# Nine pairs of row tiles multiplied by one level of Strassen, in a newly searched order

## The chip, the cores and the metric

The kernel runs on one core of one Trainium2 chip. The metric is device time in microseconds: the median of the runs of one kernel. The core has five engines that run their own instruction streams and wait for one another by semaphores: TensorE (PE, matmuls, with the weight load shown apart as PEld), VectorE (DVE), ScalarE (ACT), GpSimd (POOL) and SyncE (SP), whose queue issues the DMAs.

## The reference

Linear attention over 8 batches, 8 heads, 576 rows and 64 columns a head, followed by a feed-forward layer on the 4608 rows of 512 columns.

```python
q_s = exp(q - max(q, -1)); q_s = q_s / (sum(q_s, -1) + 1e-09)
k_s = exp(k - max(k, 2));  k_s = k_s / (sum(k_s, 2) + 1e-09)
kv  = einsum('bhsd,bhse->bhde', k_s, v)
x   = einsum('bhsd,bhde->bhse', q_s, kv)         # then 4608 rows of 512
h   = x @ w_in                                   # 512 -> 1024
e   = exp(h - max(h)); solu = h * e / (sum(e) + 1e-09)
ln  = (solu - mean(solu)) / sqrt(var(solu) + 1e-06) * g_ln
out = ln @ w_out                                 # 1024 -> 512
```

All arrays are f32.

## The kernel before

The 4608 rows are 36 row tiles of 128 (`tiles`): four of each batch, and one that the rests of two batches share, named by batch and number and counted in order (tile 13 is (3, 0), tile 27 is (6, 0)). The first four (`whole`) are computed in f32. For all others each operand of the large products is split into a high and a low f16 part, and a product is three f16 products (high by high, low by high, high by low).

The work is written as generators, one for each piece, cut into steps by `yield`:

- `keys` (K), `queries` (Q) and `rest_queries` (R), `load_v` (V) and others load k, q and v, form the softmaxes, and multiply k by v (L425). `scales` (S) forms hs, the scale that turns the integer-like product of scaled operands back into h.
- `attend` (x) multiplies q by kv for two row tiles at once (L613) into two PSUM banks. ScalarE copies the high half to f16 (L623), VectorE the difference (L625): the stationary operands xT of the next product.
- `hidden` (h) makes one row tile's h of 128 x 1024 in a PSUM tile of two banks: 12 terms by 2 banks are 24 matmuls of 512 columns (L648), four to a step, six steps. Behind them comes the tail: the row maximum (VectorE, L655), nm (ScalarE, L657), the exponential e (ScalarE, L661), am, pi, p and ph (one column each, on GpSimd or VectorE, L665 to L674; p always on GpSimd), h times e in place (VectorE, L677), nmu (ScalarE), u's two f16 halves (ScalarE L682, VectorE L684), a DMA transpose of u into uT (L687, SyncE's queue), the Square that sums the variance (ScalarE, L691), and four operations of one column. Square is the last to read the PSUM tile.
- `project` (o) multiplies uT by w_out: 24 matmuls of 512 columns (L722) in four steps of six, then a scaled copy to SBUF and the store.

There are two PSUM tiles for h (tag `h`, `bufs=2`), three of one bank for `attend` and others (`att`), and one for o; these are all eight banks. `weights_in_scaled` (W) splits w_in (`iw`) into `wi` once. `BUFS` holds the counts of some SBUF buffers, first that of the tag `uT`.

The order is written by hand. `ORDER` is a list of step names; `in_turns` takes them one by one and runs the next step of the named generator, so the list is the program order of each engine, and each engine works through its own instructions in that order. A name with `.v` puts those instructions of the step that pass through `on()` on VectorE instead of GpSimd or ScalarE.

Of the kernel before, what the change touches and what calls it, by code (L numbers as in the profile page):

```python
# [8 lines left out]
F32 = mybir.dt.float32  # L9
# [8 lines left out]
P = 128  # L18

BUFS = 12, 3, 2  # L20
FIRST = 3, 0, 2, 1
WHOLE = 4
ON_VECTOR = 2
ORDER = (
# [819 lines left out]
```

## Time and profile before

| | us |
|---|---|
| median of 3 runs | 457.09 |
| lowest, highest | 457.0, 457.23 |
| span of the profiled execution, first to last instruction | 455.4 |
| TensorE busy | 435.4 (96%) |
| VectorE busy | 337.5 (74%) |
| ScalarE busy | 276.0 (61%) |
| GpSimd busy | 209.2 (46%) |

The profile is of one execution. Its page gives no time for that execution other than the span, which begins with the first instruction and ends with the last; the measured time holds something more at both ends. Busy times are sums over the span. Matmuls are pipelined: the length of one in the trace is more than the distance from one to the next, and what a row of them costs is read from the chain.

### The profile page before, as it was taken

Reading aid. Unit: us, or ns where it says so; the run is one execution under the profiler, and the core shown is the slowest. Engines: PE = TensorE matmul, PEld = TensorE weight load, DVE = VectorE, ACT = ScalarE, POOL = GpSimd, SP = SyncE. Lnnn points to the kernel's source line nnn. Section 1 sums busy time; section 2 is a strip of 40 time slices with the busy share of each in tenths; the row PEclk is TensorE's granted clock in tenths of the full one; section 3 lists DMA queues with packets and bytes.
Section 4 is the critical chain, followed back from the end, with each engine's and each line's share of the span. In section 5 each row is a group of like instructions: output and inputs, shape, how many; then the busy total and the mean of one; then the engine's idle time right before and its main releaser. Section 6 shows DMA issues by size and latency. Waiting matters only on the chain.

```text
span 455.4 us, 8734 instructions
## 1 busy us (share of the span) xinstructions
PE 435.4 (96%) x3351; PEld 208.4 (46%) x3351; DVE 337.5 (74%) x619; ACT 276.0 (61%) x477; POOL 209.2 (46%) x334
## 2 busy tenths in 40 slices
PE   0898899999999999999999999999999999999996
PEld 0543344454445445444544445444454444444445
DVE  5999999989788898769967869777967565443410
ACT  3889998685866656466657566556657444441331
POOL 4107885886774355734363375712423234211120
PEclk9999999999999999999999999999999999999999
DMA  8997699699779994996884787884436425334071
GB/s 276 394 317 276 124 199 173 166 224 185 176 155 211 199 244 63 221 212 148 180 210 91 158 190 167 191 201 97 107 64 136 94 46 117 69 79 84 24 186 46
DMA packets 167082, 73.98 MB, mean 162 GB/s; under 512 B 146424, under 2 KB 155904, under 8 KB 167040
## 3 DMA queue, kind: packets, MB, share of 16 engines
q1 hardware_dynamic: 167040, 73.42, 68.7%
q8 instruction: 26, 0.43, 0.4%
q14 instruction: 16, 0.13, 0.1%
HBM read 36.70 MB, written 9.44 MB: 101 GB/s over the span
## 4 chain that ended last, share of the span: by engine, by line
PE 87%; DVE 5%; DMA 3%; ACT 3%; issue 1%; POOL 1%; ACTq 0%; DVEq 0%; POOLq 0%
PE o L722 41%; PE h L648 37%; PE x L613 4%; PE kv L425 4%; DMA w_out<-in_moe_w_out_dram 2%; DMA qm<-in_q_dram 1%; PE h L640 1%; DVE qnmx L475 1%; DVE h L677 1%; DVE iw L269 1%; PE warm_up L779 1%; DVE iw L267 0%; POOL am L665 0%; ACT qm L479 0%; ACT e L691 0%
## 5 line engine op out<-in xcount | busy, mean ns | idle before, releaser
L722 PE MATMUL o<-wo,uT 128*128 128x512 f16 (+1 forms) x888 | 198.3, 373 | 0.0
L648 PE MATMUL h<-wi,xT 128*128 128x512 f16 x768 | 177.1, 379 | 0.0
L722 PEld LDWEIGHTS <-uT 128*128 128x128 f16 x888 | 85.7, 98 | 98.0 <-issue 1.8
L648 PEld LDWEIGHTS <-xT 128*128 128x128 f16 x768 | 74.3, 98 | 89.4 <-issue 1.0
L655 DVE TENSOR_REDUCE top<-h 128x1 f32<-128x1024 f32 x36 | 43.9, 1218 | 27.6 <-PE h L648 27.4
L684 DVE SCALAR_TENSOR_TENSOR u<-h,nmu,u 128x1024 f16<-128x1024 f32 x36 | 46.0, 1277 | 15.6 <-ACT u L682 15.2
L691 ACT ACTIVATE e<-h,nmu 128x1024 f32<-128x1024 f32 x36 | 40.0, 1112 | 25.4 <-DVE u L684 25.2
L677 DVE SCALAR_TENSOR_TENSOR h<-h,ph,e 128x1024 f32<-128x1024 f32 x36 | 46.3, 1285 | 7.9 <-POOL ph L674 4.6
L665 POOL TENSOR_SCALAR am<-nm 128x1 f32<-128x1 f32 x25 | 10.3, 412 | 88.6 <-ACT nm L657 88.6
L671 POOL TENSOR_TENSOR p<-pi,mone 128x1 f32<-128x1 f32 x36 | 24.2, 671 | 55.1 <-DVE pi L668 53.5
L682 ACT ACTIVATE u<-h,nmu 128x1024 f16<-128x1024 f32 x36 | 40.1, 1113 | 1.0
L732 ACT ACTIVATE os<-o,rr 128x512 f32<-128x512 f32 (+1 forms) x23 | 15.5, 674 | 31.9 <-PE o L722 16.6
L657 ACT ACTIVATE nm<-top,hs 128x1 f32<-128x1 f32 x28 | 8.2, 294 | 43.4 <-DVE top L655 43.4
L661 ACT ACTIVATE e<-h,nm,hs 128x1024 f32<-128x1024 f32 x28 | 33.7, 1203 | 0.7
L679 ACT ACTIVATE nmu<-s 128x1 f32<-128x1 f32 x36 | 7.3, 202 | 42.0 <-DVE h L677 39.8
L640 PE MATMUL h<-iw,xT 128*128 128x512 f32 x64 | 29.8, 601 | 2.4 <-ACT e L691 2.3
L502 POOL TENSOR_TENSOR qhl<-qm,qhl 128x512 f16<-128x512 f32 x24 | 28.1, 1191 | 7.2 <-ACT qhl L162 4.6
L495 POOL TENSOR_TENSOR qm<-qm,qrec 128x1024 f32<-128x1024 f32 x12 | 23.6, 1969 | 11.7 <-DVE qrec L486 10.7
L625 DVE SCALAR_TENSOR_TENSOR xT<-x,xT 128x512 f16<-128x512 f32 (+1 forms) x36 | 22.2, 622 | 8.5 <-ACT xT L623 8.5
L477 POOL TENSOR_TENSOR qm<-qm,qnmx 128x1024 f32<-128x1024 f32 (+1 forms) x12 | 23.5, 1964 | 8.4 <-DVE qnmx L475 8.4
L730 DVE TENSOR_SCALAR os<-o,rr 128x512 f32<-128x512 f32 (+1 forms) x14 | 10.2, 728 | 20.4 <-PE o L722 20.4
L623 ACT ACTIVATE xT<-x 128x512 f16<-128x512 f32 (+1 forms) x36 | 19.2, 542 | 8.5 <-PE x L613 8.5
(155 smaller groups left out, 539.4 us busy)
## 6 DMA issues: line engine op xcount, KB each, us to landing
km<-in_k_dram SPq DMA_DIRECT2D x7, 1152.0 KB, 7.5
vm<-in_v_dram SPq DMA_DIRECT2D x28, 288.0 KB, 4.5
out_dram<-os SPq DMA_DIRECT2D x31, 256.0 KB, 3.2
qm<-in_q_dram SPq DMA_DIRECT2D x7, 1024.0 KB, 6.4
wo<-in_moe_w_in_dram SPq DMA_DIRECT2D x4, 512.0 KB, 8.6
w_in<-in_moe_w_in_dram SPq DMA_DIRECT2D x4, 512.0 KB, 9.4
wo<-in_moe_w_out_dram SPq DMA_DIRECT2D x4, 512.0 KB, 5.6
w_out<-in_moe_w_out_dram SPq DMA_DIRECT2D x4, 512.0 KB, 8.9
```

Of the source, the lines that this page charges most:

```text
L495: on(nc.gpsimd).tensor_tensor(x, x, wide(rec), op=ALU.mult)
L502: on(nc.gpsimd).tensor_tensor(lo, y, hi, op=ALU.subtract)
L640: nc.tensor.matmul(h[:, ns], xT[:, kc], iw[kc][:, ns], start=(i == 0), stop=(i == NP - 1))
L648: nc.tensor.matmul(h[:, ns], xT[:, t, kc], wi[:, s, kc, ns], start=(i == 0), stop=(i == len(terms) - 1))
L655: nc.vector.tensor_reduce(top, h, axis=AX.X, op=ALU.max, negate=True)
L661: nc.scalar.activation(e, h, AF.Exp, bias=nm, scale=hs, accum_out=z)
L671: nc.gpsimd.tensor_tensor(p, pi, mone, op=ALU.pow)
L677: nc.vector.scalar_tensor_tensor(h, h, ph, e, op0=ALU.mult, op1=ALU.mult, accum_out=s1)
L682: nc.scalar.activation(u[:, 0], h, AF.Identity, bias=nmu)
L684: nc.vector.scalar_tensor_tensor(u[:, 1], h, nmu, u[:, 0], op0=ALU.add, op1=ALU.subtract)
L691: nc.scalar.activation(e, h, AF.Square, bias=nmu, accum_out=s2)
L722: nc.tensor.matmul(o, uT[:, j, f], wo[:, s, f, cols], start=(f == 0 and j == 0 and s == 0), stop=(f == NF - 1 and j == 1))
```

## The change

The rows x of nine pairs of row tiles (tiles 13, 15, 18, 20, 22, 24, 27, 29, 31 and the one behind each: all pairs of batches 3 to 7 except the last) and w_in are seen as two by two blocks, and h of the pair is formed by one level of Strassen's scheme in Winograd's form: seven products of blocks instead of eight, each of six matmuls of 512 columns.

- `combined` takes the place of the last four steps of `attend` for these pairs. It forms the four sums of blocks of x in f32 and splits the six left operands into high and low f16 parts.
- `weights_combined` (T, 16 steps, once) forms the four sums of blocks of w_in in place in `iw` and splits them into `wt`. `iw` therefore stays in use until then, and `uT` has 13 buffers instead of 12.
- `hidden_twin` (H) holds both PSUM tiles of h for a pair, runs the seven products into their four banks, and adds them up by one copy, three additions and four additions that also return the maximum (`tensor_tensor_reduce`).
- `hidden` then runs only the tail of such a tile, without its own row maximum. Since the maximum now comes without its sign turned, hs and isc have a second column with the negative scale. The input scale goes from 2^14 to 2^13 and that of kv to 2^11 from the fourth batch on.
- `ORDER`: the first 425 steps are the same steps on the same engines (three steps at the ends of exhausted generators are left out), and the other 1334 are another sequence. The list has 1759 steps instead of 1669. In it, many steps of K and Q that were marked `.v` are not.

The diff; of the list, one line of the new one stands.

```diff
--- before.py
+++ after.py
@@ -17,82 +17,66 @@
 
 P = 128
 
-BUFS = 12, 3, 2
+BUFS = 13, 3, 2
 FIRST = 3, 0, 2, 1
 WHOLE = 4
+TWINS = 3
 ON_VECTOR = 2
 ORDER = (
...
+    "S3 h8 o8 x15 h11 h12 o8 h11 h12 Q4c Q4a o8*3 h11 x15*2 H13*7 V40 Q4c*2 o7 Q4a*3 h11 H13*2 K4 o8 h11*2 "
...
 )
 
 
@@ -138,7 +122,7 @@
     nc.vector.memset(mone, -1.0)
     one = cst.tile([P, 1], F32, name="one")
     nc.vector.memset(one, 1.0)
-    isc = cst.tile([P, 1], F32, name="isc")
+    isc = cst.tile([P, 2], F32, name="isc")
     vm = cst.tile([P, NP, KC, D + 1], F32, name="vm")
     nc.vector.memset(vm[:, :, :, D : D + 1], 1.0)
     bd = [cst.tile([P, 2, H, D], F16, name=f"bd{i}") for i in range(3)]
@@ -184,7 +168,7 @@
         nc.vector.tensor_scalar(p2.bitcast(I32), top.bitcast(I32), 0x7F800000, None, op0=ALU.bitwise_and)
         inv = sm.tile([P, 1], F32, name=f"inv_{name}", tag="inv")
         nc.vector.tensor_scalar(inv, p2, 2.0**-80, 2.0**-up, op0=ALU.max, op1=ALU.mult)
-        s = sm.tile([P, 1], F32, name=f"s_{name}", tag="s")
+        s = (cst if name == "in" else sm).tile([P, 1], F32, name=f"s_{name}", tag="s_in" if name == "in" else "s")
         nc.vector.reciprocal(s, inv)
         return s, inv
 
@@ -287,14 +271,43 @@
         yield
         wide = ps.tile([P, P], F32, name="wide_in", tag="att", bufs=3)
         yield from largest(m1, wide, "in")
-        s, inv = pow2_scale(tops["in"], 14, "in")
-        nc.vector.tensor_copy(isc, inv)
+        s, inv = pow2_scale(tops["in"], 13, "in")
+        iw["scale"] = s
+        nc.vector.tensor_copy(isc[:, 0:1], inv)
+        nc.vector.tensor_scalar(isc[:, 1:2], inv, -1.0, None, op0=ALU.mult)
         yield
         for kc in range(NP):
             nc.scalar.activation(wi[:, 0, kc], iw[kc], AF.Copy, scale=s)
             yield
             nc.vector.scalar_tensor_tensor(wi[:, 1, kc], iw[kc], s, wi[:, 0, kc], op0=ALU.mult, op1=ALU.subtract)
             yield
+
+    wt = {}
+
+    def weights_combined():
+
+        left, right = slice(0, DF // 2), slice(DF // 2, DF)
+        for j in range(2):
+            b11, b12, b21, b22 = (iw[kc][:, cols] for kc in (j, 2 + j) for cols in (left, right))
+            for out, x, y in ((b11, b12, b11), (b12, b22, b12), (b22, b22, b11), (b21, b22, b21)):
+                on(nc.gpsimd).tensor_tensor(out, x, y, op=ALU.subtract)
+                yield
+        s = iw["scale"]
+        for j in range(2):
+            t = wt[j] = sb.tile([P, 2, 2, DF], F16, name=f"wt{j}", tag="wd", bufs=WB)
+            for i in range(2):
+                x = iw[2 * i + j]
+                nc.scalar.activation(t[:, 0, i], x, AF.Copy, scale=s)
+                yield
+                nc.vector.scalar_tensor_tensor(t[:, 1, i], x, s, t[:, 0, i], op0=ALU.mult, op1=ALU.subtract)
+                yield
+
+    def right_block(name, s, i):
+
+        cols = slice(0, DF // 2) if name in ("11", "21", "t1", "t4") else slice(DF // 2, DF)
+        if name[0] == "t":
+            return wt[i][:, s, 0 if name in ("t1", "t3") else 1, cols]
+        return wi[:, s, 2 * (int(name[0]) - 1) + i, cols]
 
     gw = {"sum": cst.tile([P, NW], F32, name="gw_sum")}
 
@@ -441,7 +454,7 @@
         nc.vector.tensor_reduce(mx, kvn, axis=AX.XY, op=ALU.max, apply_absolute_value=True)
         yield
         yield from largest(mx, kv[:, 512 - P : 512], f"kv{b}")
-        s, inv = pow2_scale(tops[f"kv{b}"], 14, f"kv{b}")
+        s, inv = pow2_scale(tops[f"kv{b}"], 14 if b < TWINS else 11, f"kv{b}")
         t = bd[b % 3]
         kv_of[b] = (t, inv)
         yield
@@ -568,14 +581,17 @@
 
     def scales(b):
 
-        hs = hs_of[b] = sm.tile([P, 1], F32, name=f"hs{b}", tag="hs")
-        on(nc.gpsimd).tensor_tensor(hs, kv_of[b][1], isc, op=ALU.mult)
+        hs = hs_of[b] = sm.tile([P, 2], F32, name=f"hs{b}", tag="hs")
+        if b < TWINS:
+            on(nc.gpsimd).tensor_tensor(hs[:, 0:1], kv_of[b][1], isc[:, 0:1], op=ALU.mult)
+        else:
+            on(nc.gpsimd).tensor_tensor(hs, kv_of[b][1].broadcast_to([P, 2]), isc, op=ALU.mult)
         yield
         if b % 2 == 1:
             both = hs_of["rest", b // 2] = sm.tile([P, 1], F32, name=f"hsr{b}", tag="hsr", bufs=2)
-            nc.vector.tensor_copy(both[0:R], hs_of[b - 1][0:R])
-            yield
-            nc.vector.tensor_copy(both[R:P], hs[R:P])
+            nc.vector.tensor_copy(both[0:R], hs_of[b - 1][0:R, 0:1])
+            yield
+            nc.vector.tensor_copy(both[R:P], hs[R:P, 0:1])
             yield
 
     def attend_whole(b, c):
@@ -615,6 +631,9 @@
                         start=(m == s == i == 0), stop=(m + 1 == len(groups) and s == 1 and 2 * i + 2 == NP),
                     )
         yield
+        if row_tiles in twins:
+            yield from combined(name, row_tiles, accs)
+            return
         halves = [slice(g * NP // 2, (g + 1) * NP // 2) for g in range(2)]
         xT = sb.tile([P, 2, NP, n, P], F16, name=f"xT{name}", tag="xT", bufs=XB)
         for r, row_tile in enumerate(row_tiles):
@@ -626,14 +645,112 @@
             yield
 
 
+    left_of, done = {}, {}
+
+    def combined(name, row_tiles, accs):
+
+        t = sb.tile([P, 16 * P], F16, name=f"xT{name}", tag="xT", bufs=XB)
+        a11 = t[:, 0 : 4 * P].rearrange("p (s i k) -> p s i k", s=2, i=2)
+        side = t[:, 4 * P : 12 * P].rearrange("p (s i c k) -> p s i c k", s=2, i=2, c=2)
+        a21 = t[:, 12 * P : 16 * P].bitcast(F32).rearrange("p (i k) -> p i k", i=2)
+        x21, x11 = accs[0][:, :, 0], accs[0][:, :, 1]
+        x22, x12 = accs[1][:, :, 0], accs[1][:, :, 1]
+        sums = sb.tile([P, 4, 2, P], F32, name=f"sums{name}", tag="uT", bufs=UB)
+        split = sb.tile([P, 2, 4, 2, P], F16, name=f"split{name}", tag="uT", bufs=UB)
+        left_of[row_tiles[0]] = {
+            **{f"s{j + 1}": (lambda s, i, j=j: split[:, s, j, i]) for j in range(4)},
+        }
+        nc.scalar.activation(a21, x21, AF.Copy, scale=1.0 / QS)
+        yield
+        nc.scalar.activation(a11[:, 0], x11, AF.Copy, scale=1.0 / QS)
+        yield
+        nc.vector.scalar_tensor_tensor(sums[:, 2], x11, 1.0 / QS, a21, op0=ALU.mult, op1=ALU.subtract)
+        yield
+        nc.vector.scalar_tensor_tensor(a11[:, 1], x11, 1.0 / QS, a11[:, 0], op0=ALU.mult, op1=ALU.subtract)
+        yield
+        nc.scalar.activation(side[:, 0], accs[1], AF.Copy, scale=1.0 / QS)
+        yield
+        nc.vector.scalar_tensor_tensor(sums[:, 0], x22, 1.0 / QS, a21, op0=ALU.mult, op1=ALU.add)
+        yield
+        nc.vector.scalar_tensor_tensor(sums[:, 1], x11, -1.0 / QS, sums[:, 0], op0=ALU.mult, op1=ALU.add)
+        yield
+        nc.vector.scalar_tensor_tensor(sums[:, 3], x12, 1.0 / QS, sums[:, 1], op0=ALU.mult, op1=ALU.subtract)
+        yield
+        nc.vector.scalar_tensor_tensor(side[:, 1], accs[1], 1.0 / QS, side[:, 0], op0=ALU.mult, op1=ALU.subtract)
+        yield
+        cast(on(nc.scalar), split[:, 0], sums)
+        yield
+        on(nc.gpsimd).tensor_tensor(split[:, 1], sums, split[:, 0], op=ALU.subtract)
+        yield
+
+    def hidden_twin(row_tiles):
+
+        lefts = left_of[row_tiles[0]]
+        name = name_of(row_tiles[0])
+
+        def product(out, left, right):
+            terms = [(i, s, r) for i in range(2) for s, r in ((0, 0), (1, 0))] + [(i, 0, 1) for i in range(2)]
+            for n, (i, s, r) in enumerate(terms):
+                nc.tensor.matmul(
+                    out, lefts[left](s, i), right_block(right, r, i), start=(n == 0), stop=(n + 1 == len(terms))
+                )
+
+        vw = sb.tile([P, 2, DF // 2], F32, name=f"vw{name}", tag="uT", bufs=UB)
+        v_, w_ = vw[:, 0], vw[:, 1]
+        left, right = slice(0, DF // 2), slice(DF // 2, DF)
+        t1 = ps.tile([P, DF], F32, name=f"h{name_of(row_tiles[1])}", tag="h", bufs=2)
+        product(t1[:, left], "11", "11")
+        yield
+        t2 = ps.tile([P, DF], F32, name=f"h{name}", tag="h", bufs=2)
+        product(t2[:, left], "s2", "t2")
+        yield
+        cast(on(nc.scalar), w_, t1[:, left])
+        yield
+        product(t1[:, left], "12", "21")
+        yield
+        nc.vector.tensor_tensor(v_, t2[:, left], w_, op=ALU.add)
+        yield
+        product(t1[:, right], "s1", "t1")
+        yield
+        product(t2[:, right], "s3", "t3")
+        yield
+        product(t2[:, left], "22", "t4")
+        yield
+        tops = [sm.tile([P, 1], F32, name=f"top{name}_{i}", tag="ttop", bufs=8) for i in range(4)]
+        nc.vector.tensor_tensor_reduce(t1[:, left], t1[:, left], w_, 1.0, -3.0e38, ALU.add, ALU.max, tops[0])
+        yield
+        nc.vector.tensor_tensor(w_, t2[:, right], v_, op=ALU.add)
+        yield
+        nc.vector.tensor_tensor(v_, t1[:, right], v_, op=ALU.add)
+        yield
+        product(t1[:, right], "s4", "22")
+        yield
+        nc.vector.tensor_tensor_reduce(t2[:, left], w_, t2[:, left], 1.0, -3.0e38, ALU.subtract, ALU.max, tops[1])
+        yield
+        nc.vector.tensor_tensor_reduce(t2[:, right], t2[:, right], v_, 1.0, tops[1], ALU.add, ALU.max, tops[2])
+        done[row_tiles[0]] = t2, tops[2]
+        yield
+        nc.vector.tensor_tensor_reduce(t1[:, right], t1[:, right], v_, 1.0, tops[0], ALU.add, ALU.max, tops[3])
+        done[row_tiles[1]] = t1, tops[3]
+        yield
+
     def hidden(row_tile):
 
 
 
-        xT, name = xT_of[row_tile], name_of(row_tile)
-        h = ps.tile([P, DF], F32, name=f"h{name}", tag="h", bufs=2)
-
-        if row_tile in whole:
+        name = name_of(row_tile)
+        if row_tile in done:
+            h, top = done[row_tile]
+        else:
+            xT = xT_of[row_tile]
+            h = ps.tile([P, DF], F32, name=f"h{name}", tag="h", bufs=2)
+
+        if row_tile in done:
+            hs, minus = hs_of[row_tile[0]][:, 0:1], hs_of[row_tile[0]][:, 1:2]
+        elif row_tile in whole:
             for i, kc in enumerate(FIRST):
                 for n in range(NB):
                     ns = slice(n * 512, (n + 1) * 512)
@@ -650,11 +767,12 @@
                     )
                 if i % 2 == 1:
                     yield
-            hs = hs_of[("rest", row_tile[0] // 2) if row_tile[1] == C else row_tile[0]]
-        top = sm.tile([P, 1], F32, name=f"top{name}", tag="htop")
-        nc.vector.tensor_reduce(top, h, axis=AX.X, op=ALU.max, negate=True)
+            hs = hs_of[("rest", row_tile[0] // 2) if row_tile[1] == C else row_tile[0]][:, 0:1]
+        if row_tile not in done:
+            top = sm.tile([P, 1], F32, name=f"top{name}", tag="htop")
+            nc.vector.tensor_reduce(top, h, axis=AX.X, op=ALU.max, negate=True)
         nm = sm.tile([P, 1], F32, name=f"nm{name}", tag="nm")
-        nc.scalar.activation(nm, top, AF.Copy, scale=hs)
+        nc.scalar.activation(nm, top, AF.Copy, scale=minus if row_tile in done else hs)
         yield
         e = sb.tile([P, DF], F32, name=f"e{name}", tag="e", bufs=3)
         z = sm.tile([P, 1], F32, name=f"z{name}", tag="z")
@@ -749,6 +867,7 @@
     tiles[-2:] = tiles[:-3:-1]
     whole = tiles[:WHOLE]
     firsts = [[t] for t in tiles[:4]] + [[(b, c), (b, c + 1)] for b in range(1, B) for c in (0, 2)] + [[(b, C)] for b in range(1, B, 2)]
+    twins = [[(b, c), (b, c + 1)] for b in range(TWINS, B) for c in (0, 2)][:-1]
     works = {}
 
     ENGINES = {"v": nc.vector, "p": nc.gpsimd, "a": nc.scalar}
@@ -785,6 +904,9 @@
     for t, row_tile in enumerate(tiles):
         works[f"h{t}"] = hidden(row_tile)
         works[f"o{t}"] = project(row_tile)
+    works["T"] = weights_combined()
+    for group in twins:
+        works[f"H{tiles.index(group[0])}"] = hidden_twin(group)
     for group in firsts:
         works[f"x{tiles.index(group[0])}"] = attend_whole(*group[0]) if group[0] in whole else attend(group)
     for b in range(B):
```

## Rows read from the trace of the kernel before

**Rows 1.** The page: span; part 1, busy us; part 2, granted clock.

```profile
span 455.4 us, 8734 instructions
...
PE 435.4 (96%) x3351; PEld 208.4 (46%) x3351; DVE 337.5 (74%) x619; ACT 276.0 (61%) x477; POOL 209.2 (46%) x334
...
PEclk9999999999999999999999999999999999999999
```

**Rows 2.** The page, part 4: the chain that ended last.

```profile
PE 87%; DVE 5%; DMA 3%; ACT 3%; issue 1%; POOL 1%; ACTq 0%; DVEq 0%; POOLq 0%
PE o L722 41%; PE h L648 37%; PE x L613 4%; PE kv L425 4%; DMA w_out<-in_moe_w_out_dram 2%; DMA qm<-in_q_dram 1%; PE h L640 1%; DVE qnmx L475 1%; DVE h L677 1%; DVE iw L269 1%; PE warm_up L779 1%; DVE iw L267 0%; POOL am L665 0%; ACT qm L479 0%; ACT e L691 0%
```

**Rows 3.** Windows: stretch, length, busy us and instructions by engine, clock, DMA share.

```profile
core 0: us, PE busy (x) PEld busy (x) DVE busy (x) ACT busy (x) POOL busy (x), PEclk, DMA share, GB/s
107.00:425.00 318.00, 318.00 (x2389) 150.03 (x2387) 233.71 (x432) 180.26 (x317) 140.25 (x241) 1.00 0.67 144
```

**Rows 4.** Chain in order of time from 100 us on (start, us, what).

```profile
105.06 0.86 PE h L648 x4
...
144.19 5.18 PE o L722 x24
149.37 5.18 PE h L648 x24
...
424.76 27.27 PE o L722 x150
```

**Rows 5.** Groups by shape from 100 us on: count, busy, mean ns, idle.

```profile
L495 POOL TENSOR_TENSOR qm<-qm,qrec 128x1024 f32<-128x1024 f32 x10 | 19.8, 1982 | 11.4 <-DVE qrec L486 10.7 <-DVE den L432 0.6
...
L625 DVE SCALAR_TENSOR_TENSOR xT<-x,xT 128x512 f16<-128x512 f32 x24 | 16.4, 682 | 5.5 <-ACT xT L623 5.5
...
L623 ACT ACTIVATE xT<-x 128x512 f16<-128x512 f32 x24 | 13.9, 590 | 5.7 <-PE x L613 5.7
...
L479 ACT ACTIVATE qm<-qm 128x1024 f32<-128x1024 f32 x10 | 10.4, 1051 | 0.0
...
L677 DVE DVE_READ_ACCUMULATOR h<-h,ph,e 128x1 f32 x30 | 4.2, 139 | 0.0
...
L625 DVE SCALAR_TENSOR_TENSOR xT<-x,xT 128x256 f16<-128x256 f32 x8 | 3.2, 410 | 3.0 <-ACT xT L623 3.0
...
L623 ACT ACTIVATE xT<-x 128x256 f16<-128x256 f32 x8 | 2.9, 378 | 2.1 <-PE x L613 2.1
```

**Rows 6.** Timeline: maximum, u, Square of tile 27; maximum, Square of tile 34.

```profile
358.07 1.23 DVE L655 TENSOR_REDUCE top<-h 128x1 f32<-128x1024 f32 x1 [3.38 <-PE h L648]
...
363.83 1.28 DVE L684 SCALAR_TENSOR_TENSOR u<-h,nmu,u 128x1024 f16<-128x1024 f32 x1 [1.42 <-ACT u L682]
...
365.14 1.11 ACT L691 ACTIVATE e<-h,nmu 128x1024 f32<-128x1024 f32 x1 [1.35 <-DVE u L684]
...
411.85 1.22 DVE L655 TENSOR_REDUCE top<-h 128x1 f32<-128x1024 f32 x1 [3.54 <-PE h L648]
...
431.55 1.11 ACT L691 ACTIVATE e<-h,nmu 128x1024 f32<-128x1024 f32 x1 [3.02 <-DVE u L684]
```

**Rows 7.** Timeline: tile 18's Square and the next h matmul in its buffer.

```profile
245.45 1.11 ACT L691 ACTIVATE e<-h,nmu 128x1024 f32<-128x1024 f32 x1 [0.97 <-DVE u L684]
...
247.21 2.97 PE L648 MATMUL h<-wi,xT 128*128 128x512 f16 x13
```

**Rows 8.** Timeline near 171 us; then p's line from 100 us on.

```profile
170.82 1.21 DVE L477 TENSOR_TENSOR qm<-qm,qnmx 128x1024 f32<-128x1024 f32 x1
...
170.93 1.53 POOL L671 TENSOR_TENSOR p<-pi,mone 128x1 f32<-128x1 f32 x1
...
L671 POOL TENSOR_TENSOR p<-pi,mone x30: 549/562/1542, 107.1 to 429.6; 128x1 f32<-128x1 f32 x30
```

**Rows 9.** The page, part 6: the loads of v.

```profile
vm<-in_v_dram SPq DMA_DIRECT2D x28, 288.0 KB, 4.5
```

**Rows 10.** Waits from 107 to 425 us (us in total, times, longest).

```profile
ACT e L691 <- DVE u L684: 19.6, 18, 3.2
```

More of the change, by code (lines that the diff above doesn't have):

```diff
@@ L626, in attend @@
             yield
-    def hidden(row_tile):
-        xT, name = xT_of[row_tile], name_of(row_tile)
-        h = ps.tile([P, DF], F32, name=f"h{name}", tag="h", bufs=2)
-        if row_tile in whole:
+    left_of, done = {}, {}
[9 more added lines that the diff above has]
+        left_of[row_tiles[0]] = {
+            "11": lambda s, i: a11[:, s, i],
+            "12": lambda s, i: side[:, s, i, 1],
+            "22": lambda s, i: side[:, s, i, 0],
+            **{f"s{j + 1}": (lambda s, i, j=j: split[:, s, j, i]) for j in range(4)},
[22 more added lines that the diff above has]
+        yield
```

124 rows, old and new, of the table ORDER are left out of this document.

## The prediction

> **What bounds the kernel now.** I read the page first, for the share of each engine and the clock: TensorE is busy for 435.4 of 455.4 us, its granted clock stands at full in all 40 slices, and no other engine passes 74% [rows 1]. Then the chain of work that ended last: 87% of the span is TensorE, and the two great loops, o and h, hold 78% [rows 2]. An average can hide stages, so the windows come next: from 107 to 425 us TensorE is busy for the whole of 318.00 us [rows 3], and in order of time the chain has nothing but TensorE from 66.8 us on; a row of 24 matmuls takes 5.18 us there, so one of 512 columns costs 5.18 / 24 = 0.2158 us [rows 4] (the 379 ns that the groups show for one is its length in the pipeline, not its price). Time is thus lost by a matmul and won by a matmul, one for one, as long as TensorE doesn't wait. Today it does not wait after 67 us. VectorE works 233.71 of those 318 us, ScalarE 180.26, GpSimd 140.25 [rows 3]: all behind.
>
> **What the change removes.** Nine pairs of row tiles had 2 x 24 matmuls for h; seven products of 6 make 42. Nine times 6 is 54 matmuls, 54 x 0.2158 = 11.65 us, all from the stretch where TensorE sets the time. The first 425 steps are the old ones (105 us on TensorE [rows 4]) and no pair's product lies among them, so nothing is to be won or lost there but the one tiny instruction that writes the negated scale; the batch-0 work around it is taken as 0. If TensorE stayed full, the time would be 457.09 - 11.65 = 445.44. The median is 457.09 and the span of the profiled execution 455.4, so 1.7 us lie outside the span; they stay.
>
> **What it adds on the other engines.** Per pair, in place of two copies of 590 ns and two differences of 682 to 684 ns, `combined` has on ScalarE two copies of 256 elements (0.38 each), one of 512 (0.59) and the cast of 1024 (about 1.05, by the 1051 ns of qm), and on VectorE five operations of 256 (0.41) and one of 512 (0.68); GpSimd gets a subtraction of 1024, 1.98 us by qm [rows 5]. `hidden_twin` adds one copy (0.6), three additions of 512 (0.68 each) and four additions with a maximum, and drops two TENSOR_REDUCEs of 1.22 [rows 5, 6]. The trace holds no addition with a maximum. Its nearest rows are the 512-element operation (682 ns) plus the 139 ns accumulator read that follows h, 0.82; the far bound is the fused 1024-element pass and its read, 1.42 [rows 5]; I take 0.82, by the row of the same width. VectorE per pair: 5 x 0.41 + 0.68 + 3 x 0.68 + 4 x 0.82 - 2 x 0.68 - 2 x 1.22 = +4.3 us, or +6.7 at the far bound; ScalarE 2 x 0.38 + 0.59 + 1.05 + 0.6 - 2 x 0.59 = +1.8; GpSimd +2.0. Over nine pairs 38, 16 and 18 us. The sixteen steps `T` add four copies and four differences of 1024 (4 x 1.05, 4 x 1.28) and eight subtractions of 512. Of the stretch's 233.71 us VectorE then has at most 233.7 + 38 + 5 + 3 = 280 on 318 - 11.65 = 306 us of TensorE, so its sum is still covered; the new list also moves key and query work from VectorE to GpSimd, which rises by some 50 us (18 for the pairs, 6 for `T`, the rest moved). Sums hide it all; what costs is the order, next.
>
> **Where the cover goes.** There are two PSUM buffers for h. A buffer is taken by the first matmul of a tile and comes free when its Square has read it. The shortest tail in the trace, that of tile 27, runs from its row maximum's start at 358.07 to Square's end at 366.25, 8.2 us; the longest of the 32, started at 411.85 and ended at 432.66, is 20.8, and the median of the 32 is 12.6 [rows 6]. The first matmul into a freed buffer follows Square's end by 0.6 us where TensorE was at hand (245.45 + 1.11 to 247.21) [rows 7]; seven of 32 follow within 0.6 us, the nearest after 0.3. I counted, from the order list at 0.2158 us a matmul, the TensorE work between a tile's last matmul and the next use of its buffer. In the old list 29 reuses have 11.3 to 18.7 us, most of them 13 to 17. In the new one, from the first pair on, 23 reuses have, sorted, 8.3, 8.7, 8.8, 9.8, 10.0, 10.0, 10.0, 10.9, 10.9, 11.3, 11.3, 11.7, 11.7, 12.6 and nine from 13.5 to 22.5. Both tiles of a pair end together and stand in one another's way on VectorE and ScalarE, and the next pair needs both buffers at once. So each microsecond by which the turnaround (tail plus hand-over) passes its cover is now TensorE idle. Summed over the list: a turnaround of 8.8 costs 0.6 us, 10.0 costs 4.4, 10.8 costs 10.0, 11.2 costs 13.4, 11.6 costs 17.6.
>
> What is the turnaround of a hurried pair? The shortest old tail, 8.2, less its 1.23 for the row maximum, plus 0.82 for the addition that stands in its place, plus one operation of the other tile in the way (Square or u, 1.11 to 1.28, with two reads of 0.2: 1.6 together), plus 0.6 to hand over: 8.2 - 1.23 + 0.82 + 1.6 + 0.6 = 10.0, cost **4.4 us**. The old median is no measure: with 13 to 17 us of cover nothing hurried those tails. But it is the far bound.
>
> **Waits inside a pair.** The third product overwrites the bank that the copy must have read, and the last overwrites the bank of the third addition. Between them lie one product (1.29 us) for the 0.6 us copy, and two or more steps for the additions. With ScalarE free that is nothing; behind one operation of 1.1 us it is about 0.4. **Moved loads**: the 288 KB loads of v stand closer to the matmuls that read them; they land 4.5 us after issue [rows 9], and the smallest gaps are 1.1, 1.3, 2.4 and 3.7 us of TensorE work (5.0 in the old list). SyncE's queue runs ahead of TensorE unless a transpose in front of the load waits for its u, so the price lies between 0 and 3.4 + 3.2 + 2.1 + 0.8 = 9.5 us. For both together I take **1.6 us** (bounds 0 and about 12). The end is the same: o's last matmuls run without pause for 27.27 us [rows 4], and the new list leaves some 30 us of them after the last h.
>
> **Two engines on one port.** While VectorE runs an operation with two SBUF inputs (qm of L477), GpSimd's p takes 1.53 us in place of a median 562 ns, and p lies on every tail [rows 8]. After the shared steps I count 25 such operations of VectorE in the new list and 35 in the old one, and 50 us more work on GpSimd: the collision becomes rarer on one side and likelier on the other. I book 0 for it; its far bound is one such stretched p per pair on a tail without slack, 1 us a pair, 9 us, and it lies in the slower case. The Trainium skill (page "SBUF — State Buffer", section "Who interferes with whom") says that the shared port is held for the whole instruction by whichever starts first, and that a VectorE instruction with at most one SBUF input stays out of it (outside its two-port modes). By that rule the additions of the twins, which read PSUM and one SBUF tile, hold up nobody; the row agrees as to p, and no row shows the additions.
>
> **The forecast.** 457.09 - 11.65 + 4.4 + 1.6 = **451.4 us**: about half of the gain is given back at the hand-over of the h buffers from pair to pair. Its own range, with a loss of 3 to 11 us, is 448.4 to 456.2.
>
> **Rivals.** *Nearly everything lands*: tails are as short as 8.2 and the twins' two chains interleave without loss (turnaround 8.8 to 9.4, loss 0 to 3 us): 445.4 to 448.4. For it: the tail of tile 27 shows that 8.2 can be had [rows 6]; against it: one of 32 did it, and eleven were above 13.4. *Slower*: the two-buffer hand-over decides. From a turnaround of about 11.0 on (1.0 more than I assume, less than one more operation in the way per tail) the loss passes 11.65; at 11.6 it is 17.6, which gives 457.09 - 11.65 + 17.6 = 463.0; it is the likeliest value of this case. For it: the old median of 12.6 [rows 6]; ScalarE's waits for VectorE's u just ahead of Square, 18 of them in the old order [rows 10]; and the maxima at their far bound (0.6 more each, two on the tail) would alone do it. Against it: TensorE's stall moves all later work of TensorE as well, so one loss gives the next reuse cover, and a sum of separate shortfalls is too high. The Trainium skill (page "Trainium Kernel Development and Optimization", section "Best Practices") warns to mind PSUM pressure, since tiling TensorE's work speeds compute and not the evacuation of PSUM; that is this rival, and no run so far shows its size. *No change*: losses of 10.7 to 12.6 us. *The change doesn't do what it says* (the seven products aren't cheaper than 42 matmuls): their moving operands have 512 columns in the diff, as those of L648 have, so I give it no chance of its own.
>
> **Chances.** Forecast 0.60; nearly everything 0.13; within 0.2% 0.08; slower 0.19. A difference under about 0.2% (0.9 us) can't be told from none here. Faster by more: 0.73. The range of 8 in 10 reaches from 446.0 (under it about 0.04) to 459.5 (above it about 0.13).
>
> **What would show it.** Right: 336 matmuls at h's line and 378 in the products, 3297 in all; TensorE busy about 424 us; windows after 107 us that are no longer full, the idle time just ahead of a pair's first two products, released by ScalarE's Square; VectorE above 80%. Wrong: the windows stay full (first rival); idle inside the pair, released by ScalarE's copy or VectorE's additions, or at kv by a DMA (the 1.6 us was too little); additions with a maximum of over 1 us; a granted clock below full after a stall, which no row of before shows and which would make every matmul behind it dearer.

## The result and the profile after

The changed kernel takes **453.15 us** (453.0 to 453.33), before 457.05 beside it: ratio 0.9914 (0.99 to 0.9929), 3.9 us less. The forecast was 451.4. Of the 11.65 us of matmuls taken away, 7.75 came back as other time. The page, with the chain's share of each engine as its last line but one:

```profile
span 451.4 us, 8807 instructions
...
PE 425.3 (94%) x3297; PEld 203.3 (45%) x3297; DVE 361.5 (80%) x710; ACT 298.8 (66%) x529; POOL 261.1 (58%) x361
...
PEclk9999999999999999999999999999999999999999
...
PE 67%; DVE 14%; ACT 6%; POOL 5%; DMA 4%; issue 4%; SPq 0%; ACTq 0%; DVEq 0%; POOLq 0%
PE o L840 33%; PE h L697 17%; PE h L765 10%; PE x L629 2%; PE kv L438 2%; DVE u L802 2%; DVE h L795 2%; DMA w_out<-in_moe_w_out_dram 2%; DVE ph L792 2%; DVE qnmx L488 1%; DMA qr<-in_q_dram 1%; POOL qm L490 1%; ACT qm L492 1%; POOL qhl L515 1%; DMA qm<-in_q_dram 1%
```

Against [rows 1, 2] the matmuls are 54 fewer and the clock is the same, but TensorE's share of the chain falls from 87% to 67%, and a line stands in the chain that moves one column of 128 numbers: VectorE's ph, L792 (L674 before). The window that answers to [rows 3], where TensorE had been full, and the waits of TensorE (us in total, times, longest; the first, before 66 us, is the same in both kernels):

```profile
107.00:425.00 318.00, 312.36 (x2355) 147.01 (x2354) 261.32 (x524) 207.41 (x376) 193.99 (x278) 1.00 0.68 146
...
PE qt L560 <- POOL qn L505: 9.9, 1, 9.9
PE h L765 <- ACT e L809: 4.3, 4, 1.8
...
PE x L629 <- DVE bd L471: 0.7, 1, 0.7
...
PE o L840 <- ACT os L850: 0.5, 2, 0.3
PE h L697 <- DVE vw L727: 0.4, 2, 0.2
```

TensorE is idle for 5.6 of 318 us, and most of it waits for Square (L809) ahead of an h tile. The four waits, by the timeline, end at 126.99, 146.53, 215.24 and 319.71 us: ahead of tiles 10, 11, 17 and 26, which are all single tiles, two of them before any pair begins. No wait for Square stands ahead of a pair's product (L697). The added operations cost what was booked; the groups by shape from 100 us on, which answer to [rows 5]:

```profile
L792 DVE TENSOR_TENSOR ph<-p,hs 128x1 f32<-128x1 f32 x9 | 11.4, 1264 | 1.5 <-POOL p L789 1.5
...
L733 DVE CUSTOM_DVE_ANT_0 h<-h,vw,top 128x512 f32<-128x512 f32 x9 | 6.8, 758 | 0.3
...
L723 DVE CUSTOM_DVE_ANT_0 h<-h,vw 128x512 f32<-128x512 f32 x9 | 6.2, 690 | 1.7 <-PE h L697 1.7
...
L733 DVE DVE_READ_ACCUMULATOR2_ANT top<- 128x1 f32 x9 | 1.3, 141 | 0.0
```

An addition with a maximum takes 0.69 to 0.76 us and its read 0.14. The odd row is ph: 1264 ns for one column. The timeline ahead of the longest wait of the four shows why (start, us, engine, line):

```profile
206.64 0.55 POOL L789 TENSOR_TENSOR p<-pi,mone 128x1 f32<-128x1 f32 x1 [1.45 <-DVE pi L786]
207.16 5.20 POOL L424 TENSOR_TENSOR km<-km,kb 128x1152 f32<-128x1152 f32 x2
207.22 2.57 DVE L792 TENSOR_TENSOR ph<-p,hs 128x1 f32<-128x1 f32 x1
...
209.90 1.29 DVE L795 SCALAR_TENSOR_TENSOR h<-h,ph,e 128x1024 f32<-128x1024 f32 x1
...
213.98 1.11 ACT L809 ACTIVATE e<-h,nmu 128x1024 f32<-128x1024 f32 x1 [0.30 <-DVE u L802]
...
215.24 1.02 PE L765 MATMUL h<-wi,xT 128*128 128x512 f16 x4 [1.82 <-ACT e L809]
```

p ends on GpSimd, GpSimd takes the next instruction of its queue, a 2.6 us operation on km (the row merges two of them), and 0.06 us later VectorE starts ph, which multiplies two columns from SBUF. ph ends when that operation ends. Everything behind it is late by 2.4 us, and TensorE stands idle for 1.82. The same is seen at 109, 119, 132 and 312 us, with operations of 1.9 or 2.6 us. These five ph are longer than 0.16 us each by 10.0 us in total; the other four take 0.15 to 0.16.

### The profile page after: what moved, and what is told of

It reads as the page before. It is cut to its first block, busy times and chain, and to the rows that moved or that the text cites. A ratio compares the mean times of both kernels' runs of the same rounds, so it can differ in the third digit from the quotient of the medians.

```text
span 451.4 us, 8807 instructions
## 1 busy us (share of the span) xinstructions
PE 425.3 (94%) x3297; PEld 203.3 (45%) x3297; DVE 361.5 (80%) x710; ACT 298.8 (66%) x529; POOL 261.1 (58%) x361
## 4 chain that ended last, share of the span: by engine, by line
PE 67%; DVE 14%; ACT 6%; POOL 5%; DMA 4%; issue 4%; SPq 0%; ACTq 0%; DVEq 0%; POOLq 0%
PE o L840 33%; PE h L697 17%; PE h L765 10%; PE x L629 2%; PE kv L438 2%; DVE u L802 2%; DVE h L795 2%; DMA w_out<-in_moe_w_out_dram 2%; DVE ph L792 2%; DVE qnmx L488 1%; DMA qr<-in_q_dram 1%; POOL qm L490 1%; ACT qm L492 1%; POOL qhl L515 1%; DMA qm<-in_q_dram 1%
## 5 line engine op out<-in xcount | busy, mean ns | idle before, releaser
L840 PE MATMUL o<-wo,uT 128*128 128x512 f16 (+1 forms) x888 | 194.2, 373 | 0.5 <-ACT os L850 0.5
L765 PE MATMUL h<-wi,xT 128*128 128x512 f16 x336 | 75.8, 379 | 4.3 <-ACT e L809 4.3
L765 PEld LDWEIGHTS <-xT 128*128 128x128 f16 x336 | 32.4, 98 | 44.0 <-issue 5.7
L850 ACT ACTIVATE os<-o,rr 128x512 f32<-128x512 f32 (+1 forms) x31 | 21.0, 676 | 39.5 <-PE o L840 32.3
L809 ACT ACTIVATE e<-h,nmu 128x1024 f32<-128x1024 f32 x36 | 40.0, 1114 | 9.9 <-DVE u L802 9.6
L697 PE MATMUL h<-wt,split 128*128 128x512 f16 x162 | 37.9, 379 | 0.0
L424 POOL TENSOR_TENSOR km<-km,kb 128x1152 f32<-128x1152 f32 x13 | 34.5, 2662 | 4.8 <-issue 3.6
L490 POOL TENSOR_TENSOR qm<-qm,qnmx 128x1024 f32<-128x1024 f32 (+1 forms) x16 | 30.0, 1882 | 11.8 <-DVE qnmx L488 11.6
L697 PEld LDWEIGHTS <-split 128*128 128x128 f16 x216 | 21.0, 98 | 25.9 <-issue 1.2
L773 DVE TENSOR_REDUCE top<-h 128x1 f32<-128x1024 f32 x18 | 21.9, 1217 | 10.0 <-PE h L765 10.0
L822 POOL TENSOR_TENSOR r<-var,mhalf 128x1 f32<-128x1 f32 x36 | 21.2, 592 | 13.3 <-DVE var L819 12.4
```

Source lines behind the costliest of these rows:

```text
L424: on(nc.gpsimd).tensor_tensor(km[:, ns], km[:, ns], wide, op=ALU.subtract)
L490: on(nc.gpsimd).tensor_tensor(x, x, wide(nmx), op=ALU.add)
L697: nc.tensor.matmul(out, lefts[left](s, i), right_block(right, r, i), start=(n == 0), stop=(n + 1 == len(terms)))
L765: nc.tensor.matmul(h[:, ns], xT[:, t, kc], wi[:, s, kc, ns], start=(i == 0), stop=(i == len(terms) - 1))
L809: nc.scalar.activation(e, h, AF.Square, bias=nmu, accum_out=s2)
L840: nc.tensor.matmul(o, uT[:, j, f], wo[:, s, f, cols], start=(f == 0 and j == 0 and s == 0), stop=(f == NF - 1 and j == 1))
```

## Experiments

**One operand less for ph.** Theory A: the waits come from this collision. Theory B, the forecast's: the list hands over the two h buffers too late, whatever ph costs.

```diff
-        on(nc.gpsimd).tensor_tensor(ph, p, hs, op=ALU.mult)
+        (nc.vector.tensor_scalar(ph, p, hs, None, op0=ALU.mult) if on(nc.gpsimd) is nc.vector else nc.gpsimd.tensor_tensor(ph, p, hs, op=ALU.mult))
```

> The changed kernel with ph, where it runs on VectorE, as one tensor times a per-partition scalar instead of two tensors; nothing else moves. Theory A (the stalls come from the port that VectorE and GpSimd share: nine such ph took 11.4 us in the changed kernel, the longest 2.58 us, just ahead of the TensorE waits at 116, 127, 215 and 320 us): each ph falls to about 0.15 to 0.2 us, the four waits of TensorE for Square (4.3 us by the waits) shrink to under 1.5 us together, and the time falls from 453.15 to 448.5 to 450.5. Theory B (the hand-over of the two h buffers is too tight in the list itself, whatever ph costs): the time stays within 0.5 us of 453.15 and the waits stay.

Measured: **447.2 us** (447.19 to 447.5), 0.9783 of before (0.9768 to 0.9798), 6.0 us below the changed kernel. ph (min/median/max ns) and the waits of TensorE:

```profile
L792 DVE TENSOR_SCALAR ph<-p,hs x9: 202/213/214, 109.2 to 385.1; 128x1 f32<-128x1 f32 x9
...
PE o L840 <- ACT os L850: 0.5, 2, 0.3
PE kv L438 <- ACT km L426: 0.4, 1, 0.4
PE h L697 <- DVE vw L727: 0.4, 2, 0.2
```

All four waits for Square are gone (the expectation names 116 us as one of them; that wait is x's for bd, and the fourth for Square ends at 146.53). Theory B falls, and the gain is more than A's own range (448.5 to 450.5). The 0.7 us ahead of x (bd stands behind the same late ph on VectorE) went with them, and each wait costs more than its idle time. Set matmul by matmul beside this run, the changed kernel falls back by 0.94, 0.51, 1.98 and 1.54 us at waits of 0.77, 0.35, 1.82 and 1.37: 0.16 more each, since idle time is counted from the end of the matmul before, 0.38 us behind its start, while the next would have started 0.22 behind it. With 0.99 at x and a step of 0.13 behind it that makes 6.1 us.

**Square from SBUF, alone and with the first edit.** Square reads the rounded high half of u in place of h, so the h buffer comes free one operation earlier.

```diff
-        nc.scalar.activation(e, h, AF.Square, bias=nmu, accum_out=s2)
+        nc.scalar.activation(e, u[:, 0], AF.Square, accum_out=s2)
```

> The changed kernel with Square reading the high half of u in SBUF instead of h in PSUM; the variance is then that of the rounded u. An h buffer comes free after VectorE's u instead of after Square, some 1.3 us earlier, with all ph as they are. Both theories let the four waits for Square shrink, by up to 1.3 us each: 0.4 + 0.8 + 1.3 + 1.3 = 3.7 us at most, so 449.4 to 451. If the hand-over is not what TensorE waits for, the time stays at 453.15.

> Both edits at once. If port and hand-over are the same stalls seen from two ends, the gains don't add: 447.5 to 449 and no TensorE wait over 0.5 us ahead of h. The floor with no stall at all is 445.4.

Measured: 451.21 alone, 447.62 with both. An earlier hand-over softens the waits while ph is late and has nothing to give once it isn't. From the first split-f16 h matmul to the end of the last matmul, both edits together take 369.0 us and the first alone 369.0; what the two lose against the one lies before that (0.8 us between the two profiled executions).

**The products undone in the new order.** The pairs' xT as before, 48 matmuls a pair in the seven product steps (7, 7, 7, 7, 7, 7, 6), both buffers taken as early as in the twins, two row maxima in the last two steps:

```diff
-        if row_tiles in twins:
-            yield from combined(name, row_tiles, accs)
-            return
...
+        chunks = {
+            0: [(1, left, 7)], 1: [(0, left, 7)], 3: [(1, left, 5), (0, left, 2)], 5: [(0, left, 3), (1, right, 4)],
+            6: [(1, right, 2), (0, right, 5)], 7: [(0, right, 7)], 11: [(1, right, 6)],
+        }
```

> The new order with the products undone: the nine pairs form h by 48 matmuls as before, spread over the seven product steps of the order, with the old copies of x and two row maxima. The additions, sums and their copies are gone; the combined weights are still formed, but not used. TensorE gets its 11.65 us back, VectorE loses some 35 us. Forecast's mechanism (tails of the twins set the stalls): TensorE's work is back and most stalls go, 457 to 459. Rival (the stalls belong to the new order's key and query work on GpSimd, not to the twins' additions): they all stay, 453.15 + 11.65 = 464.8 at most, 461 to 464.8.

> The new order with the products undone and ph as one tensor times a scalar. If the stretched ph made the stalls of the plain products too, they go and what is left is the 11.65 us of matmuls: 447.2 + 11.65 = 458.9, 458 to 460. If the plain products have stalls of their own in this order (both row maxima stand at the end of the pair), 460 to 466.

Measured: 469.74, and 462.5 with ph as one tensor times a scalar. Against 447.2 the 54 matmuls are worth 15.3 us here: 11.65 of their own, the rest waits of 3.04 and 1.10 us for Square, where the row maxima stand late in this order. So the new order without the products is no gain in this form (462.5 against 457.1), but most of its loss is those two waits, and the same with the maxima placed earlier was not tried. 469.74 is more than either theory gave: it has the waits of the changed kernel as well, and after two of its waits TensorE ran slower. Windows of it at the longer and at the shorter one, then of the run of 462.5 (columns as in [rows 3]):

```profile
215.00:219.40 4.40, 0.94 (x5) 0.30 (x4) 2.64 (x5) 3.97 (x7) 0.00 (x0) 0.97 0.00 1
219.40:222.00 2.60, 2.57 (x7) 0.89 (x7) 1.83 (x4) 2.60 (x4) 0.59 (x3) 0.50 1.11 224
222.00:226.00 4.00, 4.00 (x19) 1.71 (x17) 1.42 (x3) 1.36 (x3) 3.82 (x8) 0.94 0.88 182
...
331.20:334.00 2.80, 2.79 (x8) 1.02 (x8) 2.33 (x5) 1.64 (x3) 2.64 (x6) 0.60 1.01 192
...
212.00:216.00 4.00, 0.96 (x6) 0.33 (x4) 2.61 (x3) 3.70 (x6) 0.00 (x0) 1.00 0.01 3
216.00:219.00 3.00, 3.00 (x15) 1.35 (x15) 1.76 (x4) 2.73 (x4) 0.96 (x4) 1.00 1.12 233
```

**The dose.** Every ph on VectorE, as two tensors, in both kernels:

```diff
-        on(nc.gpsimd).tensor_tensor(ph, p, hs, op=ALU.mult)
+        nc.vector.tensor_tensor(ph, p, hs, op=ALU.mult)
```

> The dose, on the kernel before: every ph on VectorE as two tensors, so that more of them meet a long GpSimd operation. If what decides is tail against cover, the old order's cover (11 to 18 us) takes a ph of up to 2.6 us: 457.1 to 458. If a stretched ph costs TensorE by itself, the time rises by some us.

> The same dose on the changed kernel: every ph on VectorE as two tensors. There GpSimd works some 50 us more and the cover is 8 to 12 us at most reuses. Theory of port and cover: more stretched ph, more and longer waits of TensorE for Square, 456 to 466. If the port isn't the cause, the time stays near 453 (the move takes ph out of GpSimd's queue, which by itself helps).

> The kernel before with the same edit of ph, where it runs on VectorE. Its few stretched ph (at most 1.10 us) lie on tails that have 11 to 18 us of cover, and TensorE never waits, so the theory of cover gives 457.1, no change within 0.2%. If the edit gave something by itself on every order, the kernel before would fall by 1 us or more too.

Measured: 463.76 from before, 473.94 from the changed kernel, and 457.12 for before with ph as one tensor times a scalar (ratio 1.0, 0.9991 to 1.0009). The first is not what I expected, and its trace says where: three of the four ph of the f32 tiles, before 82 us, became 1.26 to 2.48 us long, TensorE's wait for Square there grew from 2.3 to 4.6 us, a wait of 1.8 for VectorE came up, and the first split-f16 h matmul starts at 78.01 instead of 72.93 us. So the old order is tight at its start, too. From there to the end of the last matmul it takes 380.5 us, before 379.1: 1.4 us more. The changed kernel takes 390.5 from there, against 375.1: 15.4 more. ph in before, in the first run (two rows) and in the second, and TensorE's waits for Square in the second:

```profile
L674 DVE TENSOR_TENSOR ph<-p,hs x8: 149/159/1103, 117.0 to 430.2; 128x1 f32<-128x1 f32 x8
...
L674 DVE TENSOR_TENSOR ph<-p,hs x28: 108/160/2564, 91.0 to 436.7; 128x1 f32<-128x1 f32 x28
L674 DVE TENSOR_TENSOR ph<-p,one x4: 151/1486/2483, 39.7 to 81.1; 128x1 f32<-128x1 f32 x4
...
L792 DVE TENSOR_TENSOR ph<-p,hs 128x1 f32<-128x1 f32 x28 | 25.2, 899 | 6.4 <-POOL p L789 6.4
...
PE h L697 <- ACT e L809: 5.0, 5, 1.6
PE h L765 <- ACT e L809: 4.4, 4, 1.8
```

More collisions, more time, and far more of it in the new order. After 82 us the old order has 6 stretched ph of 32, together 7.5 us too long (each set against 0.16), and loses 1.4; the new one has 14, 24.0 us too long, and loses 15.4, of which 1.7 are matmuls at a lower clock (last section). The edit also takes 27 ph out of GpSimd's queue and puts them into VectorE's, and no run did that with the short form, so the place in the queue may have a part in both numbers. The edit that gives 6.0 us in the new order gives nothing in the old one; there nine ph run on VectorE (the eight of the row and one of two batches' rests), with a median of 159 ns and two of 993 and 1103, so only 1.8 us too long.

**How tight the new order is.** ph as one tensor times a scalar, and a second Square (1.1 us) ahead of the real one on tiles from 13 on; the same second Square in the kernel before; and, apart from that, the short ph with five matmuls in a product instead of six (one of the high-by-low terms is left out, so h is less exact). The second Square:

```diff
-        nc.scalar.activation(e, h, AF.Square, bias=nmu, accum_out=s2)
+        (nc.scalar.activation(e, h, AF.Square, bias=nmu) if tiles.index(row_tile) >= 13 else None, nc.scalar.activation(e, h, AF.Square, bias=nmu, accum_out=s2))
```

> The changed kernel with ph as one tensor times a scalar, and on tiles from 13 on a second Square ahead of the real one that keeps the h buffer 1.1 us longer. Theory of cover: with the reuses' slack as it is (0.14 to 2.9 us), taking the worse of a pair, 7 us of new waits, at most 14.6: 453 to 460. If the tails have room, under 449.

> The same second Square on the same tiles of the kernel before. Seven reuses there have less than 1.1 us of slack, together 2.8 us short at most: 457.1 to 460. If the old order is as tight as the new one, it rises as much as the other does.

> The changed kernel with ph as one tensor times a scalar, and one of the six matmuls of each product left out (the last of the high-by-low terms, so h is less exact): 63 matmuls, 13.6 us of TensorE. If TensorE still sets the time with room behind it, 447.2 - 13.6 = 433.6. If the tails are as close behind as the slack after Square suggests (13 of 30 reuses of an h buffer follow Square by 0.6 us or less), most of it comes back as waits: 438 to 446.

Measured: 460.36, which is 13.2 us above 447.2; 460.44, which is 3.3 above before; and 436.62, 10.6 less for 13.6 us of matmuls. The waits for Square after 66 us, of the first run and then of the second:

```profile
PE h L697 <- ACT e L809: 10.1, 12, 1.8
...
PE h L765 <- ACT e L809: 0.8, 2, 0.6
...
PE h L648 <- ACT e L691: 2.1, 4, 0.7
```

The same 1.1 us costs the new order four times what it costs the old one, and now at the pairs' first products, where the forecast had looked for it. The expectation of 7 us, the worse buffer of each pair, was too low: both buffers of a pair made TensorE wait, one after the other. The old order's 3.3 us are also a little more than the 2.8 expected of it. The third run lies between its two expectations and says that the other engines have some room still: most of 13.6 us landed, and no wait for Square after 66 us is over 0.15 us.

## Why the prediction was right, and where it wasn't

**The time and the sign** were right, 1.75 us off and inside its own range; the way to them was right in one half, and that the total fits is luck.

- *What the change removes.* 54 matmuls, 11.65 us: confirmed. From the first split-f16 h matmul to the end of the last matmul, before takes 379.09 us, the new order with the short ph 369.00: 10.09 less, so 1.56 us of it are lost, to four waits of 0.21 to 0.26 us and the 0.16 more at each.
- *What it adds elsewhere* was sized well: additions with a maximum at 0.83 to 0.90 with their read (0.82 booked), VectorE at 261.3 us in the stretch (280 at most).
- *Waits inside a pair and moved loads*, 1.6 us: the sum is the 1.56 above, but only half of it is what was described, two waits of a product for VectorE's addition (0.4 us idle). The other half are two waits of o for its scaled copy by ScalarE (0.5), which the prediction doesn't name. The loads of v cost nothing: no wait for them is in the trace.
- *The cover*, 4.4 us: TensorE's waits for Square are 4.3 us, but for another reason and in another place, ahead of single tiles and not of a pair's first two products. With ph short there are none. The failed step is the one turnaround of 10.0 us for all 23 reuses. In the run of 447.2 the tails of the twins are 8.2 to 20.7 us long with a median of 10.8, by which the sum over the list would give 10 us and more, and TensorE waits for none of them. A tail is short where its cover is: the order gives each just what it needs. In that run the first matmul follows Square's end within 0.6 us at 12 of 30 reuses (the expectation of the run of 436.62 says 13), 0.14 us at the least. 0.14 is also the hand-over itself, booked at 0.6: at all four waits of the changed kernel h starts 0.14 us after Square. That the hand-over is the tight place was right, as the second Square shows; that it had to cost something by itself was wrong.
- *Two engines on one port*, booked at 0: this is the term that was mis-sized, **6.0 us**. I counted VectorE's long operations as those that hold up GpSimd's p and found fewer of them. The other direction was left out: GpSimd's long operation holds up VectorE's ph. It is no matter of chance either: ph waits for p, so that GpSimd is free at that very moment, and if its next instruction is a long one it is ahead, by 0.06 us at four of the five and by 0.7 at the one where VectorE was busy. The old trace had the sign of it, two ph of 993 and 1103 ns beside a median of 159. Both lists could have been searched for a `.v` on ph with a long GpSimd step next in the queue. The Trainium skill ("SBUF — State Buffer", "Who interferes with whom") has this direction as well: whoever starts first holds the port, and a VectorE instruction with two SBUF inputs contends with a GpSimd instruction that reads SBUF. The runs agree, 2.57 us for two tensors, 0.21 with a per-partition scalar. I had applied it to p and the additions only.
- *The range.* Its upper end, 456.2, stands for a loss of 10.7 us and not of the 11 beside it, which would be 456.4; nothing hangs on it.
- *Rivals.* The first (nearly everything lands) is what the new order does once ph is short: 447.2, within its 445.4 to 448.4. The slower one was near: a second Square of 1.1 us puts the time at 460.4, and its point of decision had been set at 1.0 us a turnaround.

The two errors, 4.4 booked for a hand-over that costs nothing by itself and 0 for a port that cost 6.0, nearly cancelled.

## What to carry to other kernels

When an order is searched until its cover is used up, look for operations whose length depends on what another engine is doing, however small they are: on such an order most of their stretch is paid, on a looser one little of it. Here 10.0 us of stretch cost 6.0; in the old order 1.8 cost nothing and, behind its start, 7.5 cost 1.4. A small VectorE operation that waits for GpSimd should take one tensor from SBUF and its second factor as a per-partition scalar; here that is one line and 6.0 us. A total that fits is no proof of its terms: test each booked term by itself.

## What was not expected of the hardware

After the waits of 3.50 and 2.00 us in the run of 469.74 the granted clock read 0.50 in the next 2.6 us and 0.60 in the next 2.8, so the lower level (1.2 GHz) for part or all of them, and the 24 matmuls of h behind each took 6.84 and 7.03 us instead of 5.34. After waits of 3.04 us (the run of 462.5) and 1.82 us (the changed kernel) it stayed at 1.00. In the run of 473.94 it fell after shorter ones. Behind waits of 0.74, 0.47, 0.59 and 0.78 us within 14 us, the last two 1.4 us apart with only small matmuls of x between them, it read 0.66 and then 0.50 (columns as in [rows 3]):

```profile
166.90:168.50 1.60, 1.60 (x5) 0.59 (x6) 1.47 (x5) 1.60 (x3) 0.98 (x4) 0.66 1.13 213
168.50:170.50 2.00, 2.00 (x6) 0.76 (x5) 1.94 (x7) 1.23 (x3) 0.00 (x0) 0.50 0.71 193
```

The 24 matmuls of h from 166.90 on took 7.03 us. The length of the wait alone doesn't decide it; what does was not tried. Besides, ph on VectorE takes 0.20 to 0.21 us as a tensor times a scalar and 0.15 to 0.16 as two tensors when nothing collides, so the form that is safe is the longer one by 0.05 us.
